# Attention stage of a three-stage kernel: 65-column products in two column halves, per-head fp32 projections on 64 rows, output transposes one step later

## The chip, the cores and the metric

The kernel runs on one core of a Trainium2 chip. The metric is the device time of one execution in microseconds; lower is better. The engines of a core have names of their own in the profile: PE is the matrix engine (TensorE), PEld its weight loads, DVE the vector engine, ACT the scalar engine, POOL GpSimd, and SP the engine whose queue issues nearly all DMAs here. PE's two operands are called stationary (loaded first, by a weight load) and moving (streamed through). An accumulator bank is one of the eight banks of PSUM, into which PE writes and from which DVE and ACT read.

## The reference, cut to what matters

Three stages follow each other: feature-map attention, a dense mixture of experts weighted by a Sinkhorn matrix, and a routed mixture of experts. Only the first is touched by the change.

```python
# batch 4, heads 8, seq 576, head_dim 64, features 128
def phi(x):
    proj = np.einsum('bhsd,df->bhsf', x, w_phi)
    proj = proj - np.max(np.abs(proj), axis=-1, keepdims=True)
    return np.concatenate([np.exp(proj), np.exp(-proj)], axis=-1)
q_p, k_p = phi(q), phi(k)
kv = np.einsum('bhsf,bhsd->bhfd', k_p, v)
z = np.sum(k_p, axis=2)
num = np.einsum('bhsf,bhfd->bhsd', q_p, kv)
den = np.einsum('bhsf,bhf->bhs', q_p, z)[..., None] + 1e-06
x = num / den            # then x goes to _moe_ref and _moe2_ref
```

## The kernel before

**Units, groups, chunks.** The attention stage is cut into 8 units (`NU`): one unit is two batches of one pair of heads, 1152 tokens. A unit has 9 chunks of 128 tokens, in `NG` = 5 groups (`CH`): four groups of two chunks and a last one of a single chunk. Chunk 4 holds the end of one batch and the start of the other.

**One step.** The main loop makes one `step` per group. In it the k side works on group i and the q side on a group four steps further back, so that the q side of a unit runs while the k side of the next unit does. The helpers a step calls, with their lines:

- `proj` (L144 to L164), once for k and once for q: projects the two heads of a pair at once. The features matrix stands twice on the diagonal of `wphi`, 256 columns wide. Inputs and matrix are split into a high and a low part (`split_in`, L116: ACT casts, POOL subtracts; `wbh`, `wbl`), and three fp32r products per chunk are added up: L151, L152, L153. DVE then takes the largest magnitude of each row and head (L155) and subtracts it (L157). On the k side ACT takes the two exponentials (L161).
- `kvm` (L166): products of the exponentials of k (stationary, 128 features) with v and a column of ones (moving, 65 columns: 64 and the sum z), per chunk, sign and head (L176). They accumulate in banks C and B over the unit; at its end ACT copies them out as `kvz` (L180).
- `qtr` (L183): transposes of the subtracted projections of q through PE (L190), into a bank D; ACT takes the exponentials from there (L192).
- `num` (L195): products of the exponentials of q (stationary, 128 tokens) with `kvz` (moving, 65 or 130 columns), into a bank D (L205). DVE adds a small number to the denominators (L219), inverts (L220) and multiplies (L223), which gives `xn`.
- `xtr` (L226): transposes `xn` through PE (L232) into a bank A, ACT copies it (L234), and SP writes it to DRAM (L236).

**Order within a step.** Each engine works its instructions off in the order in which the program issues them. Without a `turn` the order is `qtr`, `proj` of k, `proj` of q, `kvm`, then `xtr` for the group whose `num` was in the last step, then `num`. In one step of five (`turn`, where the last group of a unit is summed) `kvm` comes first and q is projected before k. In DVE's queue the two projections' work stands ahead of the division of the same step.

**Banks.** Tag A has 4 banks, D has 2, B and C one each; tiles of one tag take them in turn. `qtr` and `num` alternate on the two D banks, `proj` and `xtr` share the four A banks.

**End of the stage.** In the last four steps and the two that flush the pipeline (`tail`) there is no k work; q projections go to bank C, `xtr` to B, and pieces of the second stage's first products (`fill`, `p1_group`, L583, lines L429 to L431 with 384 columns) are put between.

Of the kernel before, what the change touches and what calls it, by code (L numbers as in the profile page):

```python
# [11 lines left out]
F32 = mybir.dt.float32  # L12
F32R = mybir.dt.float32r
# [3 lines left out]
ALU = mybir.AluOpType  # L17
# [27 lines left out]
def build(tc, a, out):  # L45
# [23 lines left out]
    def f32(ap):  # L69
        return ap.bitcast(F32)  # L70
# [28 lines left out]
    CH = [(0, 1), (2, 3), (4, 5), (6, 7), (8,)]  # L99
    S2 = 2 * S  # L100
    W = D + 1

    def load_in(u, which, g):
        bp, h_ = units[u]
        cs = slice(CH[g][0] * P, (CH[g][-1] + 1) * P)
        r = ap_.tile([P, 2 * P], F32, tag="r" + which, bufs=3, name=f"r{which}{u}{g}")
        SP.dma_start(out=r[:, 0:cs.stop - cs.start], in_=a[which + "T"][bp, h_, :, cs])
        live["r" + which, u, g] = r

# [3 lines left out]
        SP.dma_start(out=v, in_=a["v"][bp, h_])  # L113
        live["v", u] = v

    def split_in(u, which, g):  # L116
        r = live.pop(("r" + which, u, g))
        n = len(CH[g]) * P
        bufs = 3 if which == "k" else 2
        hi = ap_.tile([P, 2 * P], F32R, tag="h" + which, bufs=bufs, name=f"h{which}{u}{g}")  # L120
        lo = ap_.tile([P, 2 * P], F32R, tag="l" + which, bufs=bufs, name=f"l{which}{u}{g}")
        A.copy(hi[:, :n], r[:, :n])
        (V if u == 0 else G).tensor_tensor(out=lo[:, :n], in0=r[:, :n], in1=f32(hi[:, :n]), op=ALU.subtract)
        live["s" + which, u, g] = (hi, lo)

    def warm(n):
        ps = psum("D", [P, P])
        for _ in range(n):
            T.matmul(ps, ident, ident, start=True, stop=True)

    wphi = ap_.tile([P, 2 * P], F32, bufs=1, name="wphi")
    V.memset(wphi, 0.0)
    for g in range(2):
        SP.dma_start(out=wphi[g * D:(g + 1) * D, g * P:(g + 1) * P], in_=a["w_phi"])
    for g in range(3):
        load_in(0, "k", g)
    load_v(0)
    warm(10)
    wbh = ap_.tile([P, 2 * P], F32R, bufs=1, name="wbh")
    wbl = ap_.tile([P, 2 * P], F32R, bufs=1, name="wbl")  # L140
    V.tensor_copy(wbh, wphi)
    V.tensor_tensor(out=wbl, in0=wphi, in1=f32(wbh), op=ALU.subtract)

    def proj(u, which, g):  # L144
        hi, lo = live.pop(("s" + which, u, g))
        n = len(CH[g])
        ps = psum("C" if live.get("tail") else "A", [P, 2 * n, P])
        for c in range(n):
            o = ps[:, 2 * c:2 * c + 2, :].rearrange("p h f -> p (h f)")
            cs = slice(c * P, (c + 1) * P)  # L150
            T.matmul(o, hi[:, cs], wbh, start=True, stop=False)  # L151
            T.matmul(o, hi[:, cs], wbl, start=False, stop=False)  # L152
            T.matmul(o, lo[:, cs], wbh, start=False, stop=True)  # L153
        m = ap_.tile([P, 4], F32, tag="m", bufs=4, name=f"m{which}{u}{g}")[:, 0:2 * n]
        V.tensor_reduce(out=m, in_=ps, axis=AX.X, op=ALU.max, apply_absolute_value=True)  # L155
        pr = ap_.tile([P, 4, P], F32, tag="pr" + which, name=f"pr{which}{u}{g}")[:, 0:2 * n]
        V.tensor_tensor(out=pr, in0=ps, in1=m.unsqueeze(2).to_broadcast([P, 2 * n, P]), op=ALU.subtract)  # L157
        if which == "k":
            ek = ap_.tile([P, 4, 2, P], F32, tag="eq" if u == 0 and g == 2 else "ek", bufs=2, name=f"ek{u}{g}")
            for sg in range(2):  # L160
                A.activation(out=ek[:, 0:2 * n, sg, :], in_=pr, func=AF.Exp, scale=1.0 - 2.0 * sg)  # L161
            live["ek", u, g] = ek
        else:
            live["pr", u, g] = pr  # L164

    def kvm(u, g):  # L166
        v, ek = live["v", u], live.pop(("ek", u, g))
        if g == 0:
            live["kv", u] = [psum(t, [P, 2, 2 * W]) for t in "CB"]
        for sg in range(2):  # L170
            for ci, c in enumerate(CH[g]):
                o, w = (0, 2 * W) if c in (0, 4) else (0, W) if c < 4 else (W, W)
                s0 = 0 if c == 0 else c + 1 if c <= 4 else c + 2
                for h_ in range(2):
                    ps = live["kv", u][h_]
                    T.matmul(ps[:, sg, o:o + w], ek[:, 2 * ci + h_, sg, :], v[:, h_, s0 * W:s0 * W + w], start=(c == 0 and sg == 0), stop=(c == 8 and sg == 1))  # L176
        if g == len(CH) - 1:
            kvz = ap_.tile([P, 2, 2, 2 * W], F32, tag="kvz", name=f"kvz{u}")
            for h_, ps in enumerate(live.pop(("kv", u))):
                A.copy(kvz[:, h_], ps)  # L180
            live["kvz", u] = kvz
# [13 lines left out]
    def num(u, g):  # L195
        eq, kvz = live.pop(("eq", u, g)), live["kvz", u]
        n = len(CH[g])
        ps = psum("D", [P, 6 * W])
        off, at_ = 0, []
        for ci, c in enumerate(CH[g]):  # L200
            o, w = (0, W) if c < 4 else (W, W) if c > 4 else (0, 2 * W)
            at_.append((off, w))
            for h_ in range(2):
                for sg in range(2):
                    T.matmul(ps[:, off:off + w], eq[:, sg, h_, ci * P:(ci + 1) * P], kvz[:, h_, sg, o:o + w], start=(sg == 0), stop=(sg == 1))  # L205
                off += w
        d = ap_.tile([P, 4], F32, tag="d", name=f"d{u}{g}")
        xn = ap_.tile([P, 4, D], F32, tag="xn", name=f"xn{u}{g}")

        def views():  # L210
            if CH[g][0] == 4:
                for b in range(2):
                    yield slice(64 * b, 64 * b + 64), ps[64 * b:64 * b + 64, 0:4 * W].rearrange("p (h e) -> p h e", h=2)[:, :, b * W:b * W + W], slice(0, 2)
                yield slice(0, P), ps[:, 4 * W:6 * W].rearrange("p (h e) -> p h e", h=2), slice(2, 4)
            else:
                yield slice(0, P), ps[:, 0:2 * n * W].rearrange("p (h e) -> p h e", h=2 * n), slice(0, 2 * n)

        for p_, v_, s_ in views():
            V.tensor_scalar_add(d[p_, s_], v_[:, :, D], 1e-6)  # L219
        V.reciprocal(d[:, 0:2 * n], d[:, 0:2 * n])  # L220
        for p_, v_, s_ in views():
            k_ = s_.stop - s_.start
            V.tensor_tensor(out=xn[p_, s_, :], in0=v_[:, :, 0:D], in1=d[p_, s_].unsqueeze(2).to_broadcast([p_.stop - p_.start, k_, D]), op=ALU.mult)  # L223
        live["xn", u, g] = xn

    def xtr(u, g):  # L226
        bp, h_ = units[u]
        xn = live.pop(("xn", u, g))
        n = len(CH[g])
        ps = psum("B" if live.get("tail") else "A", [P, n * P])  # L230
        for c in range(n):
            T.transpose(ps[:, c * P:(c + 1) * P], xn[:, 2 * c:2 * c + 2, :].rearrange("p h e -> p (h e)"), ident)  # L232
        xo = ap_.tile([P, 2 * P], F32, tag="xo", name=f"xo{u}{g}")
        A.copy(xo[:, 0:n * P], ps)  # L234
        o = bp * S2 + CH[g][0] * P
        SP.dma_start(out=xd[:, h_, o:o + n * P], in_=xo[:, 0:n * P])  # L236


    for g in range(3):
        split_in(0, "k", g)  # L240
    ones = c0.tile([P, P], F32, name="ones")
    V.memset(ones, 1.0)
    trif = wp.tile([P, 1024], F32, tag="wA11_1", name="trif")[:, 0:P]
# [384 lines left out]
            if bg:  # L628
                bg.popleft()()

    dk, dq, dx = deque(), deque(), deque()
    filled = [0]

    def step(k, q, fill=None):
        qq, xq = list(dq), list(dx)
        dq.clear()
        dx.clear()
        if k:
            dk.append(k)
        kq = [dk.popleft() for _ in range(len(dk) - (2 if k and k[0] == 0 else 1 if k else 0))]  # L640
        turn = any(t[1] == len(CH) - 1 for t in kq)
        if turn:
            for t in kq:
                kvm(*t)
        for t in qq:
            qtr(*t)
        for which, t in (("q", q), ("k", k)) if turn else (("k", k), ("q", q)):
            if t:
                proj(t[0], which, t[1])
        if q:  # L650
            dq.append(q)
        if not turn:
            for t in kq:
                kvm(*t)
        if fill:
            filled[0] += 1
            next(fill)
        for t in xq:
            xtr(*t)
        if fill:  # L660
            filled[0] += 1
            next(fill)
        for t in qq:
            num(*t)
            dx.append(t)
# [7 lines left out]
    def at_(i):  # L673
        return order[i] if 0 <= i < len(order) else None

    for i in range((NU + 1) * NG - 1):
# [22 lines left out]
        if p == 5 and g == 3:  # L699
# [4 lines left out]
            ops = x_tasks(HS[0][1], q)  # L704
            ops["load"]()
            bg.extend(ops[k_] for k_ in XFIRST)
        for which, nx in (("k", at_(i + 1)), ("q", at_(i + 2 - NG))):
            if nx and not (which == "k" and i < 2):
                split_in(nx[0], which, nx[1])
        if i == NU * NG:  # L710
            while bg:
                bgpop()
# [4 lines left out]
        if p == 3 and g == NG - 1:  # L717
            misc_trans()
        bgpop()
    while dq or dx:  # L720
        step(None, None, first)
    at.close()

# [806 lines left out]
```

## Time and profile before

| what | value |
| --- | --- |
| median of 3 runs | 2019.83 us (2019.09 to 2023.27) |
| the profiled execution | 2022.27 us, its span in the trace 2020.5 us |
| mean granted TensorE clock over the span | 0.989 |
| PE busy | 1978.7 us (98%) |
| weight loads busy | 1901.4 us (94%) |
| DVE, ACT, POOL busy | 1309.5, 869.2, 995.1 us |
| attention stage (first to last product of `num` and `kvm`) | 10.5 to about 225 us |

An engine's busy time is the union of its instructions' durations. PE's instructions overlap: the duration of one product (about 0.27 us for a short one) holds its way through the array, and the next begins long before its end. What a product costs in a dense stretch is therefore the distance between the starts of two, not its duration. One fp32 product of the program shows as two records, each with a weight load of its own; a transpose and an fp32r product show as one.

### The profile page before, as it was taken

The numbers are of one execution on the slowest core, as the hardware profiler recorded it, in microseconds if no ns is written. First come the engines' busy times: TensorE is split into PE (matmuls) and PEld (weight loads), VectorE is DVE, ScalarE is ACT, GpSimd is POOL, SyncE is SP. The second block draws the span as 40 slices with busy tenths as digits, with TensorE's granted clock in tenths as the row PEclk, the third lists the DMA queues.
The fourth block names the chain that finished last, engine by engine and source line by source line (L and its number), as shares of the span: only waits on it lengthen the run. The fifth ranks groups of instructions, "written<-read, shape, count | busy, mean of one in ns | idle before, by whom it ended". The sixth has DMA issues, their size and how long they took to land.

```text
span 2020.5 us, 31417 instructions
## 1 busy us (share of the span) xinstructions
PE 1978.7 (98%) x11715; PEld 1901.4 (94%) x11715; DVE 1309.5 (65%) x1865; ACT 869.2 (43%) x1391; POOL 995.1 (49%) x733
## 2 busy tenths in 40 slices
PE   9999999999999999999999999999999998899998
PEld 9999999999999999999999999999999988778886
DVE  6766656466566656656665675666567444889996
ACT  5566432233333423333342333334233233777775
POOL 1255112575664747566474756647475432323332
PEclk9999999999999999999999999999999998999999
DMA  4344543543726345372644537364453344153851
GB/s 122 113 148 158 222 180 152 143 175 113 251 88 218 131 153 183 114 249 90 218 132 152 182 116 250 88 217 133 151 183 109 128 170 123 35 178 108 291 199 61
DMA packets 118979, 314.61 MB, mean 156 GB/s; under 512 B 11466, under 2 KB 65948, under 8 KB 118822
## 3 DMA queue, kind: packets, MB, share of 16 engines
q1 hardware_dynamic: 114726, 302.04, 44.8%
q0 software_dynamic: 4096, 10.51, 1.7%
q8 instruction: 95, 1.56, 0.3%
q14 instruction: 62, 0.51, 0.1%
HBM read 335.80 MB, written 32.28 MB: 182 GB/s over the span
## 4 chain that ended last, share of the span: by engine, by line
PE 76%; POOL 8%; DVE 6%; issue 5%; DMA 2%; ACT 2%; SPq 1%; POOLq 0%; DVEq 0%; ACTq 0%
PE Q L430 15%; PE Q L429 14%; PE Q L431 14%; PE psD L205 3%; PE psD L429 2%; PE psD L430 2%; PE psD L431 2%; POOL w1S L349 2%; PE psA L429 2%; PE psA L1140 2%; PE psA L431 2%; PE psA L430 2%; PE psA L1141 2%; POOL hB L477 2%; PE psA L1139 2%
## 5 line engine op out<-in xcount | busy, mean ns | idle before, releaser
L493 DVE TENSOR_TENSOR acca<-acca,Q 128x768 f32<-128x768 f32 x182 | 168.5, 949 | 133.3 <-PE Q L431 133.3
L429 PE MATMUL Q<-hT,w2S 128*128 128x384 f32 x468 | 157.5, 336 | 4.1 <-DVE rd L489 4.1
L477 POOL TENSOR_TENSOR hB<-rb,hB 128x768 fp32r<-128x768 f32 x39 | 72.1, 1848 | 180.4 <-ACT hB L474 180.4
L429 PE MATMUL Q<-xT,w1S 128*128 128x384 f32 x468 | 156.4, 334 | 0.9 <-ACT ra L498 0.9
L430 PE MATMUL Q<-hT,w2S 128*128 128x384 f32 x468 | 156.4, 334 | 0.0
L431 PE MATMUL Q<-hT,w2S 128*128 128x384 f32 x468 | 156.4, 334 | 0.0
L431 PE MATMUL Q<-xT,w1S 128*128 128x384 f32 x468 | 156.3, 334 | 0.0
L430 PE MATMUL Q<-xT,w1S 128*128 128x384 f32 x468 | 156.3, 334 | 0.0
L349 POOL TENSOR_TENSOR w1A<-raw,w1A 128x512 fp32r<-128x512 f32 x48 | 62.1, 1294 | 159.4 <-ACT w1A L348 86.2
L493 DVE TENSOR_TENSOR accb<-accb,Q 128x768 f32<-128x768 f32 x91 | 84.3, 949 | 68.0 <-PE Q L431 68.0
L1113 DVE TENSOR_TENSOR s1l<-rw,s1h 128x1024 fp32r<-128x1024 f32 x88 | 112.4, 1332 | 9.6 <-ACT s1h L1112 7.4
L489 DVE TENSOR_TENSOR Q<-Q,ra 128x768 f32<-128x768 f32 x39 | 37.7, 967 | 124.6 <-PE Q L431 124.6
L498 ACT COPY ra<-Q 128x768 f32<-128x768 f32 x39 | 31.3, 802 | 176.0 <-PE Q L431 156.3
L429 PE MATMUL Q<-xB,w1A 128*128 128x384 f32 x312 | 104.3, 334 | 0.7 <-DVE accb L851 0.7
L431 PE MATMUL Q<-hB,w2A 128*128 128x384 f32 x312 | 104.3, 334 | 0.0
L431 PE MATMUL Q<-xB,w1A 128*128 128x384 f32 x312 | 104.2, 334 | 0.0
L430 PE MATMUL Q<-xB,w1A 128*128 128x384 f32 x312 | 104.2, 334 | 0.0
L429 PE MATMUL Q<-hB,w2A 128*128 128x384 f32 x312 | 104.2, 334 | 0.0
L430 PE MATMUL Q<-hB,w2A 128*128 128x384 f32 x312 | 104.2, 334 | 0.0
L477 POOL TENSOR_TENSOR hT<-ra,hT 128x768 fp32r<-128x768 f32 x39 | 72.0, 1845 | 64.2 <-ACT hT L474 64.2
L477 POOL TENSOR_TENSOR hT<-rd,hT 128x768 fp32r<-128x768 f32 x39 | 72.3, 1854 | 57.0 <-ACT hT L474 57.0
L1079 POOL DMA_INDIRECT xgs<-x2d,idt x22 | 35.6, 1619 | 126.3 <-DVE gt L1077 126.0
(431 smaller groups left out, 6702.9 us busy)
## 6 DMA issues: line engine op xcount, KB each, us to landing
xT<-xpd SPq DMA_DIRECT2D x120, 768.0 KB
rw<-in_moe_w SPq DMA_DIRECT2D x176, 512.0 KB
xB<-xpd SPq DMA_DIRECT2D x90, 768.0 KB
raw<-in_moe_w SPq DMA_DIRECT2D x34, 512.0 KB
gate<-gd SPq DMA_DIRECT2D x45, 384.0 KB
rx<-in_moe_w SPq DMA_DIRECT2D x30, 512.0 KB
xpd<-xT SPq DMA_DIRECT2D x12, 768.0 KB
xpd<-xB SPq DMA_DIRECT2D x9, 768.0 KB
```

Of the source, the lines that this page charges most:

```text
L205: T.matmul(ps[:, off:off + w], eq[:, sg, h_, ci * P:(ci + 1) * P], kvz[:, h_, sg, o:o + w], start=(sg == 0), stop=(sg == 1))
L349: eng.tensor_tensor(out=t[:, 1], in0=r(nm), in1=f32(t[:, 0]), op=ALU.subtract)
L429: T.matmul(bank, w[:, 0, j, k, :], x[:, 0, k, :], start=start and k == 0, stop=False, skip_group_check=True)
L430: T.matmul(bank, w[:, 0, j, k, :], x[:, 1, k, :], start=False, stop=False, skip_group_check=True)
L431: T.matmul(bank, w[:, 1, j, k, :], x[:, 0, k, :], start=False, stop=stop and k == 1, skip_group_check=True)
L477: eng.tensor_tensor(out=hb[nm][:, 1], in0=src, in1=f32(hb[nm][:, 0]), op=ALU.subtract)
L489: V.tensor_tensor(out=out, in0=x, in1=y, op=op)
L493: V.tensor_tensor(out=z, in0=z, in1=ps, op=op)
L1113: V.tensor_tensor(out=lo, in0=r, in1=f32(hi), op=ALU.subtract)
L1139: T.matmul(ps[hf], th[:, k, :], wh[:, cs], start=(k == 0), stop=False)
L1140: T.matmul(ps[hf], tl[:, k, :], wh[:, cs], start=False, stop=False)
L1141: T.matmul(ps[hf], th[:, k, :], wl[:, cs], start=False, stop=(k == KD - 1))
```

## The change

Four things change in the attention stage. The products of `kvm` and `num` are issued in two halves of 64 stationary columns each (`HALVES`), which write to partitions 0 to 63 and 64 to 127 of the bank. The projections are plain fp32 products, one per chunk and head, on the 64 rows of that head; the split of inputs and matrix is gone, and each head has a bank of its own, so that DVE reads 256 columns at a time and twice as often. `xtr` moves from behind `kvm` to a place ahead of the projections, works on a group one step older (`late`; in the tail it doesn't wait a step), and takes a D bank. The raw inputs have four buffers for three, since the projection reads them itself.

```diff
     W = D + 1
+    HALVES = (slice(0, 64), slice(64, P))
 
     def load_in(u, which, g):
...
-        r = ap_.tile([P, 2 * P], F32, tag="r" + which, bufs=3, name=f"r{which}{u}{g}")
+        r = ap_.tile([P, 2 * P], F32, tag="r" + which, bufs=4, name=f"r{which}{u}{g}")
...
-    def split_in(u, which, g):
-        r = live.pop(("r" + which, u, g))
-        n = len(CH[g]) * P
-        bufs = 3 if which == "k" else 2
-        hi = ap_.tile([P, 2 * P], F32R, tag="h" + which, bufs=bufs, name=f"h{which}{u}{g}")
-        lo = ap_.tile([P, 2 * P], F32R, tag="l" + which, bufs=bufs, name=f"l{which}{u}{g}")
-        A.copy(hi[:, :n], r[:, :n])
-        (V if u == 0 else G).tensor_tensor(out=lo[:, :n], in0=r[:, :n], in1=f32(hi[:, :n]), op=ALU.subtract)
-        live["s" + which, u, g] = (hi, lo)
...
-    wphi = ap_.tile([P, 2 * P], F32, bufs=1, name="wphi")
-    V.memset(wphi, 0.0)
+    wphi = ap_.tile([P, P], F32, bufs=1, name="wphi")
     for g in range(2):
-        SP.dma_start(out=wphi[g * D:(g + 1) * D, g * P:(g + 1) * P], in_=a["w_phi"])
+        SP.dma_start(out=wphi[g * D:(g + 1) * D, :], in_=a["w_phi"])
...
-    wbh = ap_.tile([P, 2 * P], F32R, bufs=1, name="wbh")
-    wbl = ap_.tile([P, 2 * P], F32R, bufs=1, name="wbl")
-    V.tensor_copy(wbh, wphi)
-    V.tensor_tensor(out=wbl, in0=wphi, in1=f32(wbh), op=ALU.subtract)
 
     def proj(u, which, g):
-        hi, lo = live.pop(("s" + which, u, g))
+        r = live.pop(("r" + which, u, g))
         n = len(CH[g])
-        ps = psum("C" if live.get("tail") else "A", [P, 2 * n, P])
+        ps = [psum(t_, [P, n, P]) for t_ in ("CB" if live.get("tail") else "AA")]
         for c in range(n):
-            o = ps[:, 2 * c:2 * c + 2, :].rearrange("p h f -> p (h f)")
-            cs = slice(c * P, (c + 1) * P)
-            T.matmul(o, hi[:, cs], wbh, start=True, stop=False)
-            T.matmul(o, hi[:, cs], wbl, start=False, stop=False)
-            T.matmul(o, lo[:, cs], wbh, start=False, stop=True)
+            for h_ in range(2):
+                hs = slice(h_ * D, h_ * D + D)
+                T.matmul(ps[h_][:, c, :], r[hs, c * P:(c + 1) * P], wphi[hs, :], start=True, stop=True)
         m = ap_.tile([P, 4], F32, tag="m", bufs=4, name=f"m{which}{u}{g}")[:, 0:2 * n]
-        V.tensor_reduce(out=m, in_=ps, axis=AX.X, op=ALU.max, apply_absolute_value=True)
         pr = ap_.tile([P, 4, P], F32, tag="pr" + which, name=f"pr{which}{u}{g}")[:, 0:2 * n]
-        V.tensor_tensor(out=pr, in0=ps, in1=m.unsqueeze(2).to_broadcast([P, 2 * n, P]), op=ALU.subtract)
+        for h_ in range(2):
+            mh = m.rearrange("p (c h) -> p h c", h=2)[:, h_]
+            V.tensor_reduce(out=mh, in_=ps[h_], axis=AX.X, op=ALU.max, apply_absolute_value=True)
+            V.tensor_tensor(out=pr.rearrange("p (c h) f -> p h c f", h=2)[:, h_], in0=ps[h_], in1=mh.unsqueeze(2).to_broadcast([P, n, P]), op=ALU.subtract)
...
-                    T.matmul(ps[:, sg, o:o + w], ek[:, 2 * ci + h_, sg, :], v[:, h_, s0 * W:s0 * W + w], start=(c == 0 and sg == 0), stop=(c == 8 and sg == 1))
+                    for cs in HALVES:
+                        T.matmul(ps[cs, sg, o:o + w], ek[:, 2 * ci + h_, sg, cs], v[:, h_, s0 * W:s0 * W + w], start=(c == 0 and sg == 0), stop=(c == 8 and sg == 1))
...
-                    T.matmul(ps[:, off:off + w], eq[:, sg, h_, ci * P:(ci + 1) * P], kvz[:, h_, sg, o:o + w], start=(sg == 0), stop=(sg == 1))
+                    for cs in HALVES:
+                        T.matmul(ps[cs, off:off + w], eq[:, sg, h_, ci * P + cs.start:ci * P + cs.stop], kvz[:, h_, sg, o:o + w], start=(sg == 0), stop=(sg == 1))
...
-        ps = psum("B" if live.get("tail") else "A", [P, n * P])
+        ps = psum("D", [P, n * P])
...
+        if not live.get("tail"):
+            xq, late[:] = list(late), xq
+        else:
+            xq, late[:] = late + xq, []
...
         for t in qq:
             qtr(*t)
+        for t in xq:
+            xtr(*t)
...
+        if fill:
+            filled[0] += 1
+            next(fill)
         if not turn:
             for t in kq:
                 kvm(*t)
-        if fill:
-            filled[0] += 1
-            next(fill)
-        for t in xq:
-            xtr(*t)
...
-        for which, nx in (("k", at_(i + 1)), ("q", at_(i + 2 - NG))):
-            if nx and not (which == "k" and i < 2):
-                split_in(nx[0], which, nx[1])
```

## Rows read from the trace of the kernel before

**Rows 1.** Busy time by engine in stretches: length, then engine (instructions), clock, DMA share, GB/s.

```profile
70.00:95.00 25.00, 25.00 (x227) 25.00 (x226) 17.57 (x41) 15.19 (x39) 6.55 (x10) 1.00 0.35 105
...
195.00:228.00 33.00, 31.89 (x242) 31.36 (x241) 19.95 (x50) 17.91 (x42) 13.08 (x11) 1.00 0.30 108
```

**Rows 2.** Chain of waits in order of time: start, length, what sets the end.

```profile
100.24 1.73 PE psD L205 x16
105.80 1.74 PE psD L205 x16
...
125.30 1.73 PE psD L205 x16
...
204.42 1.73 PE psD L205 x16
...
209.67 1.73 PE psD L205 x16
```

**Rows 3.** Timeline of one full step on PE, and DVE's division in it: start, length.

```profile
100.08 1.90 PE L205 MATMUL psD<-kvz,eq 128*128 128x65 f32 x16
...
101.81 0.61 PE L190 MATMUL psD<-ident,prq 128*128 128x128 f32 x4
...
102.17 0.36 PE L151 MATMUL psA<-wbh,hk 128*128 128x256 f32 x1
...
102.53 0.15 DVE L219 TENSOR_SCALAR d<-psD 128x4 f32<-128x4 f32 x1
...
102.71 0.18 DVE L220 RECIPROCAL d<-d 128x4 f32<-128x4 f32 x1
...
102.92 0.42 DVE L223 TENSOR_TENSOR xn<-psD,d 128x256 f32<-128x256 f32 x1
...
103.27 0.68 DVE L155 TENSOR_REDUCE mk<-psA 128x4 f32<-128x512 f32 x1
...
103.68 0.39 PE L176 MATMUL psC<-v,ek 128*128 128x130 f32 x2
...
105.42 0.39 PE L232 MATMUL psA<-ident,xn 128*128 128x128 f32 x2
105.64 1.56 PE L205 MATMUL psD<-kvz,eq 128*128 128x65 f32 x13
```

**Rows 4.** Timeline of weight loads, third stage: eight products with 8 moving columns.

```profile
1639.93 1.03 PEld L897 LDWEIGHTS psC<-enT,acca 128*128 128x128 f32 x8
1640.88 0.19 PEld L429 LDWEIGHTS psD<-hT,w2A 128*128 128x128 f32 x1
```

**Rows 5.** Timeline of PE, third stage: two bf16 products and what follows.

```profile
1623.22 0.20 PE L931 MATMUL psC<-oh,tri 128*128 128x48 bf16 x1
1623.26 0.18 PE L932 MATMUL psC<-ohc,onesb 128*128 128x48 bf16 x1
1623.29 0.43 PE L429 MATMUL psA<-xB,w1S 128*128 128x384 f32 x1
```

**Rows 6.** Timeline of PE and loads around three transposes that use 16 rows.

```profile
232.35 0.34 PE L431 MATMUL psD<-hB,w2A 128*128 128x384 f32 x1
232.62 0.26 PEld L763 LDWEIGHTS psC<-ident,accb 16*128 16x128 f32 x3 [0.25 <-issue]
...
232.91 0.46 PEld L756 LDWEIGHTS psB<-xB,wgs 128*16 128x16 f32 x4
```

**Rows 7.** Instruction groups by shape, 0 to 420 us: busy, mean ns of one, idle before.

```profile
L123 POOL TENSOR_TENSOR lk<-rk,hk 128x256 fp32r<-128x256 f32 x28 | 20.6, 734 | 79.4 <-ACT hk L122 61.5 <-PE psD L205 11.2 <-PE psA L153 5.3
L223 DVE TENSOR_TENSOR xn<-psD,d 128x128 f32<-128x128 f32 x16 | 4.7, 292 | 0.5
L157 DVE TENSOR_TENSOR prk<-psA,mk 128x256 f32<-128x256 f32 x8 | 3.4, 425 | 0.8
L155 DVE TENSOR_REDUCE mk<-psA 128x2 f32<-128x256 f32 x8 | 3.3, 412 | 0.0
```

**Rows 8.** Waits, 5 to 228 us: who waited for whom, in total, times, longest.

```profile
DVE d L219 <- PE psD L205: 39.6, 31, 2.3
```

More of the change, by code (lines that the diff above doesn't have):

```diff
@@ L236, in xtr @@
         SP.dma_start(out=xd[:, h_, o:o + n * P], in_=xo[:, 0:n * P])
-    for g in range(3):
-        split_in(0, "k", g)
     ones = c0.tile([P, P], F32, name="ones")
@@ L629, in bgpop @@
                 bg.popleft()()
-    dk, dq, dx = deque(), deque(), deque()
+    dk, dq, dx, late = deque(), deque(), deque(), []
     filled = [0]
@@ L719, in build @@
         bgpop()
-    while dq or dx:
+    while dq or dx or late:
         step(None, None, first)
```

## The prediction

> **What bounds the kernel now.** I read the busy time by stretches first, then the chain of waits, then the timeline of one step, and last the shapes of instructions. In a steady unit PE and its weight loads are busy for all of the 25 us at the full granted clock of 2.4 GHz (1.00), DVE for 17.57 and ACT for 15.19 [rows 1]. The chain runs from `num` to `num`, 5.56 us apart for a full step, one in which all groups have two chunks; a whole unit of five steps takes 125.30 - 100.24 = 25.06 us [rows 2]. In the timeline the same full step falls into 16 records of `num`, 1.73 us; four transposes, 0.36; two projections of six products each, 102.17 to 103.68, 1.51; 16 records of `kvm`, 1.74; two output transposes, 0.22 [rows 3]. That is 5.56: PE is the bound and nothing else is. DVE waits for PE, 39.6 us in all ahead of the division alone [rows 8].
>
> What paces PE in the 65-column products is the weight load. A record of 65 or of 130 columns costs 0.108 us from start to start; eight products with only 8 moving columns cost 0.95 / 8 = 0.119 each [rows 4]. Eight columns or 65, the price is that of loading 128 stationary columns.
>
> **The split in halves.** Each record becomes two with 64 stationary columns: 64 records in a full step for 32. Call the price of one P. If loads of the two halves go one after the other, each costs half of the old one, P = 0.054, and nothing is won. If the two halves of the array load and work beside each other, the issue of instructions is the floor: two bf16 products with loads of their own follow each other after 0.04 and 0.03 us [rows 5], so P = 0.035. No row of this trace has a split product. I take 0.035: rows 5 show that PE can start products that closely, and the two halves share neither columns nor output partitions. Both ends stay for the range.
>
> **The projections.** Per chunk 3 records become 4 (two heads, two records each). At the old load price, R = 0.108, a full step pays 16 x 0.108 = 1.73 for 1.51. If the heads, on different rows, run side by side, R = 0.054 and it is 0.86. I take 0.054 by the same choice as for P; 0.108 stays as the other end. The casts on ACT and the subtractions on POOL (0.734 us each [rows 7]) vanish. I cost that at nothing: neither engine stands on a steady step's chain, and PE's full 25 us cover ACT's 15.19 and POOL's 6.55 [rows 1]. Inputs are now needed in their own step instead of the one before, with the same lead in the queue and a fourth buffer, so loads come no later than now; SP's order changes only in that the output's write stands one step later, two steps before the next stage asks for it.
>
> **Switches of the array's use.** Three transposes on 16 rows stand between full products: 232.35 to 232.91 is 0.56 us, less 0.18 for the product ahead and 3 x 0.06 for themselves, so some 0.2 for going in and out; the load wasn't pulled ahead and waited 0.25 [rows 6]. I take 0.1 for a switch. The new step has three: to 64 rows, to 64 columns, back to transposes. The Trainium skill (TensorEngine Tiling (Array Packing), Key Properties) says that a change of tiling mode drains the engine. Rows 6 agree for rows; for column halves no row shows it. Were a drain a product's whole way, 0.28, the sum below would be 0.18 x 35 steps = 6 us longer.
>
> **DVE.** It now takes each projection in two pieces. A reduction of 256 columns lasts 0.412 and a subtraction 0.425 [rows 7]; an instruction begins about 0.07 before the end of the one ahead (102.92 + 0.42 against 103.27 [rows 3]), so a pair costs 0.77. A full step has four, 3.08, and the division, 102.53 to 103.27, 0.74. DVE's own work grows to 3.82 of the step.
>
> **The moved transposes.** This is where a new wait arises. `qtr`, `xtr` and `num` now take the two D banks in turn, three per step. So `xtr` always gets the bank of the `num` just ahead of it, and must wait until DVE has divided out of it, though the data that it transposes are a step old. Before, `xtr` stood behind `kvm` in another bank. Behind the waiting `xtr` in PE's queue stand both projections, and for those waits DVE. On ACT the copy of `xtr` now stands ahead of k's exponentials, which `kvm` needs only a step later: no cost. So DVE, the engine with the growing work, idles in each step from the end of the division: 0.07 to that end, 0.05 for the signal (an estimate: 0.03 lies between dependent DVE instructions, 102.53 + 0.15 to 102.71 [rows 3], and across engines a little more), 0.22 transposes, 0.10 switch, five record distances of the first head's projection at 0.054, 0.27, and the last record's way, 0.28. Together 0.99.
>
> **The sum.** DVE's chain, full step: 3.08 + 0.74 + 0.99 = 4.81, against 5.56. PE's chain, from the last record of `num`: 0.28 its way, 0.04 signal, 0.81 division (the four transposes of `qtr` hide in these 1.13), 0.05, 0.22, two switches 0.20, 16 R and 64 P: 1.60 + 0.86 + 2.24 = 4.70. DVE's is the longer by a little. Two of the five steps have a one-chunk group: its pairs are about 0.50 (0.292 for a 128-column operation [rows 7], 0.28 for the reduction by an estimate along the same slope, less 0.07), so 2 x 0.77 + 2 x 0.50 + 0.74 + 0.99 = 4.27. The group with chunk 4 is divided in three pieces for one: 2 x 0.15 + 3 x 0.29 - 0.42 = 0.75 more. A unit: 3 x 4.81 + 2 x 4.27 + 0.75 = 23.7 for 25.06, -1.3; seven units, -9.3.
>
> First unit: it has only k work. 72 records of `kvm` at 0.11 become 144 at 0.035, 7.9 against 5.0 us; the load of v and DVE's longer pairs stand beside it, so between -2.9 and 0: I take -1.5. Tail: a full step is 5.25 [rows 2], of which 0.36, half of 1.51, 0.22 and 1.73 are known, leaving 2.18 for the inserted pieces. After: 1.13 + 0.05 + 0.22 + 0.20 + 8 x 0.054 + 2.18 + 32 x 0.035 = 5.33. The wait, which the inserted pieces covered before, eats what `num` gains. Six steps and the flush: +1, between -1 and +5. Sum: -9.8. Against the profiled execution's own 2022.27 us that is 2012.5; the runs' median lies 2.44 under that execution, which makes 2010.
>
> **The rivals.** *The halves don't overlap* (slower). P = 0.054: PE's chain in a full step is 1.60 + 3.46 + 0.86 = 5.92, or 6.79 with R = 0.108. A unit: five times 1.38 for wait, signal and switches, less 1.0 in the `turn` step, where `kvm` stands ahead and covers the wait; 1.0 for `xtr`; 72 R; 288 x 0.054 = 15.6; 0.75: 27.2 or 31.1, so +2.1 or +6.0, times seven +15 or +42; the tail adds 4 or 5. 2039 to 2067. It decides from P = 0.048 on, where 64 P eats the 3.10 us that a full step has for it. For it: the load's price goes by columns, and half the columns twice is the same. Against it: rows 5. The Trainium skill (TensorE: Matmul & The Clock Gate, The mechanism) has a weight load overlap with products in flight only where the row group differs; column halves share all rows, so by that rule it is this rival. The steady unit's loads and products, all on the same 128 rows and both busy for 25.00 us [rows 1], don't bear it out in that form.
>
> *The gain is given back* (no change). The halves overlap, yet R stays 0.108, where PE's chain is 1.60 + 1.73 + 2.24 = 5.57, the step of now; or P lies near 0.045. 2016 to 2024.
>
> *The wait doesn't bite* (faster still). If the bank were free in time, DVE's work alone would set the step, 3.82 and 3.28: a unit of 18.8, PE's 19 beside it, -6 each, about 1980. Against it: the order of banks in the program leaves no way round.
>
> **How the numbers follow.** Forecast 0.45, with its own range 2000 to 2017; halves without overlap 0.33; given back 0.15; wait that doesn't bite 0.07. Two runs of this kernel can be told apart from about 0.2%, 4 us. Faster: nine tenths of the first, the last, and a little of the third, 0.50. Same: the rest of the first and most of the third, 0.15. Slower: 0.35. The range leaves out the last case (0.07) and the upper part of the second, about 0.13: 1992 to 2046. The likeliest is 2010.
>
> **What would show it.** Right: starts of split records 0.03 to 0.04 us apart; PE idle ahead of `xtr` by some 0.7 us with DVE's division as the releaser; DVE above 75% in a steady unit, its idle time ahead of the first reduction; unit 23 to 25 us. Wrong: split records at 0.054 or more, projections at 0.108, or no idle time ahead of `xtr`.

## The result, and the profile after

The changed kernel takes 2037.67 us (2037.11 to 2038.38, four runs) beside 2019.93 for the kernel before on the same chip: ratio 1.0085, 95% interval 1.0067 to 1.0102. It is 17.7 us slower, where 10 us faster was forecast. The time lies inside the range given, on the side that the rival of the halves without overlap was to explain. That rival isn't what happened, so it is luck that the range holds: its upper part was there for another cause.

The page of the kernel after, two lines of it:

```profile
span 2036.0 us, 33944 instructions
...
PE 1956.4 (96%) x13011; PEld 1850.7 (91%) x13011; DVE 1321.3 (65%) x2012; ACT 848.5 (42%) x1311; POOL 947.4 (47%) x663
```

PE is busy for 22 us less than before and the span is 15.5 us longer: time has become idle time. The stretches show where. The first and the last line answer to [rows 1]; the middle one is one unit of five steps (columns as there).

```profile
70.00:95.00 25.00, 20.35 (x345) 17.06 (x341) 17.70 (x56) 11.67 (x26) 0.00 (x0) 0.93 0.32 97
...
76.64:104.14 27.50, 22.65 (x391) 19.34 (x391) 18.27 (x59) 12.30 (x27) 0.00 (x0) 0.94 0.43 131
...
195.00:228.00 33.00, 26.82 (x380) 22.26 (x380) 18.51 (x59) 16.65 (x35) 12.48 (x8) 0.95 0.47 170
```

PE was busy for all of 25 us; now it is for 20.35, and DVE for 17.70. Nobody is the bound: the two wait for each other in turn. The mean granted clock was 1.00 in these stretches before; now it is 0.93 to 0.95.

The timeline of the kernel after shows both halves of that (start, length; in brackets the idle time ahead and its releaser):

```profile
83.31 0.42 DVE L211 TENSOR_TENSOR xn<-psD,d 128x256 f32<-128x256 f32 x1
...
83.88 0.41 PE L220 MATMUL psD<-ident,xn 128*128 128x128 f32 x2 [0.45 <-DVE xn L211]
84.22 0.52 PEld L137 LDWEIGHTS psA<-wphi,rk 64*128 64x128 f32 x8 [0.17 <-issue]
84.22 0.71 PE L137 MATMUL psA<-wphi,rk 64*128 64x128 f32 x8
...
84.77 0.61 PE L137 MATMUL psA<-wphi,rq 64*128 64x128 f32 x8
84.96 0.42 DVE L142 TENSOR_REDUCE mk<-psA 128x2 f32<-128x256 f32 x1 [1.23 <-PE psA L137]
...
85.83 0.29 PE L163 MATMUL psC<-v,ek 128*64 128x65 f32 x4
...
86.17 0.29 PE L163 MATMUL psB<-v,ek 128*64 128x65 f32 x4
...
86.29 1.53 PE L193 MATMUL psD<-kvz,eq 128*64 128x130 f32 x32
...
87.75 0.33 PE L177 MATMUL psD<-ident,prq 128*128 128x128 f32 x1
...
90.13 0.44 PE L220 MATMUL psD<-ident,xn 128*128 128x128 f32 x2 [1.24 <-ACT eq L179]
...
100.74 0.39 PE L137 MATMUL psA<-wphi,rq 64*128 64x128 f32 x4
100.96 0.61 PE L137 MATMUL psA<-wphi,rk 64*128 64x128 f32 x8
101.51 1.15 PE L193 MATMUL psD<-kvz,eq 128*64 128x65 f32 x32
102.59 0.63 PE L177 MATMUL psD<-ident,prq 128*128 128x128 f32 x2
```

First the prices. 32 records of `num` with 65 columns take 102.59 - 101.51 = 1.08 us, 0.034 each on the average of the run (0.035 forecast, 0.108 before). Within the run they are closer: in the middle of `kvm` twelve records take 86.17 - 85.83 = 0.34, 0.028 each, and read record by record they start in pairs, two of them 0.007 us apart and the next two 0.05 later. The rest of the 1.08 is paid at the two ends of the run. Four projection records in the middle of a run take 100.96 - 100.74 = 0.22, 0.055 each (0.054); they too start in pairs. A whole projection of eight takes 0.54 or 0.55, about 0.11 more than 8 x 0.055. Record by record, this stands behind the transposes, between the first two pairs (0.21 apart, later pairs 0.11), and at the change to column halves (0.21 again); from one projection to the next nothing is paid. Where half of a group's 32 records have 130 columns, the run takes 87.75 - 86.29 = 1.46, so one of 130 columns costs (1.46 - 16 x 0.034) / 16 = 0.057: that one gains nothing by the split.

Then the wait. DVE divides at 83.31, the transposes of the older group start only at 83.88, the projections behind them at 84.22, and DVE sits idle for 1.23 us until their records are there. At 90.13 the same transposes wait for something else, for ACT's exponentials. That fits a bank from which ACT still reads the transposes of q of the same step; the trace names the releaser, not the bank. The waits of the kernel after between 20 and 245 us (us in total, times, longest):

```profile
DVE mk L142 <- PE psA L137: 32.6, 27, 1.6
...
PE psD L220 <- ACT eq L179: 18.2, 17, 1.9
PE psD L220 <- DVE xn L211: 16.6, 16, 1.9
...
DVE d L207 <- PE psD L193: 8.8, 9, 1.5
```

DVE's wait has moved from the division (39.6 us in [rows 8], and the same between 20 and 245 us; 8.8 now) to the first reduction. And in one unit, 76.6 to 104.1:

```profile
DVE mk L142 <- PE psA L137: 5.1, 4, 1.4
DVE mq L142 <- PE psA L137: 1.6, 1, 1.6
DVE d L207 <- PE psD L193: 0.8, 1, 0.8
DVE prk L143 <- ACT xo L222: 0.5, 1, 0.5
```

The clock is the last piece. In the step that ends a unit, `num` is over early, DVE still works on two projections, and PE is idle for 1.93 us, up to 77.42. Stretches of one microsecond of that step:

```profile
74.00:75.00 1.00, 1.00 (x28) 0.77 (x23) 0.97 (x4) 0.00 (x0) 0.00 (x0) 1.00 0.38 129
...
76.00:77.00 1.00, 0.00 (x0) 0.00 (x0) 0.90 (x5) 0.37 (x1) 0.00 (x0) 1.00 0.23 60
...
79.00:80.00 1.00, 1.00 (x10) 0.87 (x10) 0.72 (x2) 0.00 (x0) 0.00 (x0) 0.50 0.21 61
...
82.00:83.00 1.00, 1.00 (x32) 0.93 (x29) 0.18 (x2) 0.00 (x0) 0.00 (x0) 1.00 0.70 275
```

The granted clock falls from 2.4 GHz (1.00) to 1.2 (0.50) just after that pause, while PE is busy throughout, and is back in the last of these lines. What it costs can be read in this kernel by itself, from the starts of DVE's reciprocals in the step that follows the end of a unit: once with the fall, once, two units later, without.

```profile
76.64 0.18 DVE L208 RECIPROCAL d<-d 128x4 f32<-128x4 f32 x1
...
83.09 0.18 DVE L208 RECIPROCAL d<-d 128x4 f32<-128x4 f32 x1
...
133.47 0.18 DVE L208 RECIPROCAL d<-d 128x4 f32<-128x4 f32 x1
...
138.66 0.18 DVE L208 RECIPROCAL d<-d 128x4 f32<-128x4 f32 x1
```

6.45 against 5.19: 1.26 us for a fall. The pause of PE ahead of these two steps is the same:

```profile
77.42 0.30 PE L220 MATMUL psD<-ident,xn 128*128 128x128 f32 x1 [1.93 <-DVE xn L211]
...
134.26 0.30 PE L220 MATMUL psD<-ident,xn 128*128 128x128 f32 x1 [1.93 <-DVE xn L211]
```

So the pause alone doesn't decide. Of six such pauses at the ends of units five have a fall behind them, and of six shorter ones, 1.24 us ahead of `xtr` two steps later, two have. What else decides, no run tested. Read in stretches of two microseconds, the clock falls eight times between 50 and 220 us; in the kernel before it doesn't fall between 16 and 226 us.

The account, from the starts of the reciprocals: the first, the last of the seventh unit and the last of all, in the kernel before and in the kernel after.

```profile
26.35 0.18 DVE L220 RECIPROCAL d<-d 128x4 f32<-128x4 f32 x1
...
199.04 0.17 DVE L220 RECIPROCAL d<-d 128x2 f32<-128x2 f32 x1
...
225.09 0.17 DVE L220 RECIPROCAL d<-d 128x2 f32<-128x2 f32 x1
```

```profile
24.11 0.18 DVE L208 RECIPROCAL d<-d 128x4 f32<-128x4 f32 x1
...
211.02 0.17 DVE L208 RECIPROCAL d<-d 128x2 f32<-128x2 f32 x1
...
242.33 0.17 DVE L208 RECIPROCAL d<-d 128x2 f32<-128x2 f32 x1
```

The first division comes at 24.11 for 26.35: -2.2 (forecast -1.5). From there to the last of the seventh unit it takes 211.02 - 24.11 = 186.91 us, before 199.04 - 26.35 = 172.69: +14.2 (forecast -9.3). From there to the last division 242.33 - 211.02 = 31.31, before 225.09 - 199.04 = 26.05: +5.3 (forecast +1). Together +17.3. The -2.2 is not safely the change's: two kernels below with the same first unit have their first division at 21.44 and 22.17.

### The profile page after: what moved, and what is told of

It reads as the page before. It is cut to its first block, busy times and chain, and to the rows that moved or that the text cites. A ratio compares the mean times of both kernels' runs of the same rounds, so it can differ in the third digit from the quotient of the medians.

```text
span 2036.0 us, 33944 instructions
## 1 busy us (share of the span) xinstructions
PE 1956.4 (96%) x13011; PEld 1850.7 (91%) x13011; DVE 1321.3 (65%) x2012; ACT 848.5 (42%) x1311; POOL 947.4 (47%) x663
## 4 chain that ended last, share of the span: by engine, by line
PE 67%; POOL 9%; DVE 5%; issue 5%; ACT 1%; SPq 1%; DMA 0%; POOLq 0%; DVEq 0%; ACTq 0%
PE Q L416 14%; PE Q L417 14%; PE Q L415 14%; PE psD L415 2%; PE psD L416 2%; PE psD L417 2%; POOL w1S L335 2%; POOL hB L463 2%; PE psA L1127 2%; PE psA L1128 2%; PE psA L1126 2%; PE psD L1159 2%; PE psD L1161 2%; PE psD L1160 2%; PE psA L415 2%
## 5 line engine op out<-in xcount | busy, mean ns | idle before, releaser
L484 ACT COPY ra<-Q 128x768 f32<-128x768 f32 x39 | 31.3, 802 | 175.9 <-PE Q L417 156.2
L415 PEld LDWEIGHTS Q<-hT,w2S 128*128 128x128 f32 x468 | 87.8, 188 | 8.0 <-issue 7.9
```

The lines of the kernel that those rows point to most:

```text
L415: T.matmul(bank, w[:, 0, j, k, :], x[:, 0, k, :], start=start and k == 0, stop=False, skip_group_check=True)
```

## The experiments

Eight kernels ran. Each puts a part of the change into the kernel before, or takes one or more parts out of the changed one. All ratios are against the kernel before on the same chip (2020.3 to 2021.4 us), with their 95% intervals; a difference in us between two changed kernels is across chips, between which the kernel before differs by up to 1.5 us.

**The halves alone**, in the kernel before:

```diff
-    T.matmul(ps[:, off:off + w], eq[:, sg, h_, ci * P:(ci + 1) * P], kvz[...], ...)
+    for cs in HALVES:
+        T.matmul(ps[cs, off:off + w], eq[:, sg, h_, ci * P + cs.start:ci * P + cs.stop], kvz[...], ...)
```

(and the same in `kvm`).

> The kernel before with the split in column halves alone; projections, banks and the place of the output transposes stay as they were. Theory A (the halves pay, and what lost the time is the order of banks: the transposes' wait for the division): PE's full step falls from 5.56 by 3.47 and rises by 64 x 0.0345 = 2.2 and two switches of 0.1, to 4.5; DVE's work stays at 3.4, nothing new waits; a unit goes from 25.06 to about 20.7, seven units -30, first unit and tail -2 each: about 1986 us. Theory B (half the clock after PE's idle time is what lost it): the same sign, but PE is never idle long here, so the clock stays whole and the time is that of A. Theory C (the halves only move the wait to ACT's exponentials or DVE, whoever is next): 2010 or more.

Measured: 2005.88 us, ratio 0.9923 (0.9907 to 0.9938). The halves gain 15 us by themselves; the rival of halves without overlap is dead. They gained less than forecast. A steady unit is 21.7 to 22.6 us for the 20.7 expected, of which the 130-column records that keep their price make about 1.0 (an estimate: 24 pairs a unit at 0.11 for 0.07). Around 138 us the trace has a stall, and the clock is at half behind it, though theory B had it whole: ACT waits for a late input, and the exponentials that `num` needs stand behind that cast in ACT's queue (two lines of that timeline, and the stretch around it).

```profile
137.81 0.41 ACT L123 CAST hq<-rq 128x256 fp32r<-128x256 f32 x1 [2.85 <-DMA rq<-in_qT]
...
139.31 1.95 PE L208 MATMUL psD<-kvz,eq 128*64 128x65 f32 x26 [2.94 <-ACT eq L194]
```

```profile
120.00:145.00 25.00, 22.05 (x325) 19.99 (x320) 14.81 (x37) 17.14 (x43) 21.34 (x23) 0.87 0.64 209
```

Why that input was late (209 GB/s flow in this stretch, 118 between 45 and 70 us) no run tested.

**The old place of the output transposes, with the new bank**, in the changed kernel:

```diff
         for t in qq:
             qtr(*t)
-        for t in xq:
-            xtr(*t)
...
             for t in kq:
                 kvm(*t)
+        for t in xq:
+            xtr(*t)
```

> The changed kernel with one edit: the output transposes go back behind the k-v products, still in a D bank and still one step late. The bank that they then take was divided out of long before. Theory A: DVE's step is its own work, 4 x 0.79 + 0.83 = 4.0, with 0.1 to 0.3 of gap, PE's about 4.0; a unit of 20 to 21 us for the changed kernel's 27.5; seven units -45, about 1990 us, and PE's idle time and the half clock go with it. Theory B (the clock alone): the half clock goes, which is 1.3 us in each of seven units: about 2028. Theory C (DVE's work in twice as many pieces is the bound whatever the order): 2020 to 2030.

Measured: 2011.02 us, ratio 0.9948 (0.9933 to 0.9964). The sign is turned, but nearly half of the expected gain is missing. The wait went on to the next user of the bank: the transposes of q. In this kernel's timeline:

```profile
166.38 1.08 PE L177 MATMUL psD<-ident,prq 128*128 128x128 f32 x4 [2.34 <-DVE xn L211]
...
168.65 0.42 DVE L142 TENSOR_REDUCE mk<-psA 128x2 f32<-128x256 f32 x1 [2.42 <-PE psA L137]
```

Six such waits come to 14.0 us between 20 and 215 us, and the clock falls behind three of them. The stretch from the last division of the seventh unit to the last of all is back to 25.75 us from 31.31. At both places three tiles a step on two banks make someone wait for the division.

**Whole products in the changed kernel**, the other parts kept:

```diff
-                    for cs in HALVES:
-                        T.matmul(ps[cs, off:off + w], eq[:, sg, h_, ci * P + cs.start:ci * P + cs.stop], kvz[...], ...)
+                    T.matmul(ps[:, off:off + w], eq[:, sg, h_, ci * P:(ci + 1) * P], kvz[...], ...)
```

(and the same in `kvm`).

> The changed kernel with whole 65-column products again; the projections per head and the early transposes stay. Theory A: PE's chain of a full step becomes 1.6 + 0.3 + 0.9 + 32 x 0.108 = 6.2 and is longer than DVE's, a unit is 28 to 30 us at full clock: 2042 to 2055 us, slower than the changed kernel. If the halves themselves did the harm (theory D: switches of the array's use, or the half clock through less work on PE): 2037 or less.

Measured: 2064.11 us, ratio 1.0195 (1.0173 to 1.0217), 26 us above the changed kernel and above the 2042 to 2055 expected. So the halves are no reason for the loss. How much of the 26 us is theirs is less sure: the four executions go from 2055.5 to 2068.5 us, and the traced one, the slowest, is at half clock from 206 to 227 us besides three falls before. Its units take 28.3 to 31.3 us ahead of that. That `num` and `kvm` still count there, though PE idles, fits a step in which PE and DVE work in turn.

**More work for PE where it idles**: `num` of the turn step issued twice, with the same result.

```diff
-                for sg in range(2):
+                for sg in list(range(2)) * times:
...
-            num(*t)
+            num(*t, times=2 if turn else 1)
```

> The changed kernel, but in the one step of five where a unit is summed the numerator products are issued twice over (the first result is overwritten by the same one). They fill 1.1 of the 2.3 us for which PE stands idle there, before the clock halves. Theory B: the granted clock stays whole in most units, 1.3 us each are won: 2028 to 2031 us, though PE does more work. Theory A says nothing against it, but puts the larger part elsewhere. If the half clock costs nothing because DVE's chain hides it: 2037 to 2038, with the clock whole; if PE's added work delays the division: more.

Measured: 2035.41 us, ratio 1.0064 (1.005 to 1.0078), 2.3 us under the changed kernel, with intervals that overlap. It is a miss in the main: behind the turn the step is now mostly 5.19 us, but the falls have moved rather than gone, to six from eight after 20 us, and a step that holds one later in the unit lasts 6.98 for 5.40. Work beside the wait doesn't mend it. By the starts of the reciprocals the first division comes 1.9 us earlier, which this edit doesn't explain, the seven units are 1.7 shorter and the tail 0.8 longer. The idle time of PE that it aimed at is 1.93 us in the rows above, rather than the 2.3 expected.

**The new place, in a bank of tag A:**

```diff
-        ps = psum("D", [P, n * P])
+        ps = psum("D" if live.get("tail") else "A", [P, n * P])
```

> The changed kernel with one edit: before the tail the early output transposes take an A bank instead of a D bank; their place, ahead of the projections, stays. Theory A (the bank, not the place): their bank was read out in the step before, so they start as soon as q's transposes are through; DVE's gap of 1.1 to 1.4 per step shrinks to 0.3 or less, PE is never idle for 2 us and keeps its full clock; a unit of 27.5 falls to 20 to 22: 1988 to 2003 us. Theory E (the place: PE does the transposes while DVE has nothing, so DVE's gap stays at transposes, switch and the first projection, 1.1): 2020 or more.

Measured: 2014.94 us, ratio 0.9973 (0.9963 to 0.9982): the bank alone is worth 22.7 us, all of it in the seven units (164.1 us for 186.9); the tail, where the bank is still D, takes 31.29 for 31.31. The transposes run during the division, and after 20 us the clock falls once. But the unit is 24.08 us, not 20 to 22. Each step now takes five tiles of tag A, two for each projection and one for `xtr`, and there are four; the second projection waits for ACT's copy of `xtr`:

```profile
77.98 0.38 PE L220 MATMUL psA<-ident,xn 128*128 128x128 f32 x2
...
79.65 0.71 PE L137 MATMUL psA<-wphi,rq 64*128 64x128 f32 x6 [0.42 <-ACT xo L222]
```

Such waits come to 11.7 us in 28 steps between 20 and 200 us. The Trainium skill (TensorEngine Tiling (Array Packing), Gotcha 1: PSUM Pressure) says that different row tiles write to different banks, which makes row tiling press on PSUM; the trace agrees: two banks for a projection where there was one, five tiles a step on four banks, and this wait.

**Everything of the moved transposes undone**, halves and per-head projections kept: place and delay are those of the kernel before, and so is the bank up to the tail, where it stays D (before: B).

```diff
-        ps = psum("D", [P, n * P])
+        ps = psum("D" if live.get("tail") else "A", [P, n * P])
...
-        if not live.get("tail"):
-            xq, late[:] = list(late), xq
-        else:
-            xq, late[:] = late + xq, []
...
-        for t in xq:
-            xtr(*t)
...
         if not turn:
             for t in kq:
                 kvm(*t)
...
+        for t in xq:
+            xtr(*t)
```

> The changed kernel without its third part: output transposes at the old place, not late, in an A bank before the tail; the column halves and the projections per head stay. Theory A: like the run with the early transposes in an A bank, or a little better, since nothing stands between q's transposes and the projections: 1985 to 2003 us. If the projections in two pieces make DVE the bound (theory C): slower than the halves alone, 2006 or more, with DVE busy for over 95% of a steady unit.

Measured: 1999.3 us, ratio 0.9896 (0.9879 to 0.9912). It beats both kernels, by 21.0 and by 38.4 us. Two stretches and one reduction:

```profile
45.00:70.00 25.00, 22.37 (x401) 18.87 (x400) 22.12 (x76) 13.69 (x31) 0.58 (x1) 1.00 0.34 103
70.00:95.00 25.00, 23.41 (x429) 20.06 (x427) 20.73 (x67) 13.99 (x31) 0.00 (x0) 1.00 0.48 151
```

```profile
74.67 0.42 DVE L142 TENSOR_REDUCE mk<-psA 128x2 f32<-128x256 f32 x1 [0.38 <-PE psA L137]
```

DVE is busy for 88 and 83% of these stretches, a unit takes 22.5 us, the clock is full, and the idle time ahead of the first reduction is 0.38 us for 1.23. The stretch from the last division of the seventh unit to the last of all takes 24.68 us for 31.31. The wait of the second projection for ACT's copy is there too, but only six times between 20 and 200 us, 4.7 us in all. The Trainium skill (TensorEngine Tiling (Array Packing), PSUM Bottleneck) says that tiling speeds up TensorE but not the reading of PSUM, which may then become the limit. The trace goes that way, but not so far: DVE's share has risen from 70% [rows 1], and PE is still busy for 89 and 94%.

**The projections alone**: the kernel above with whole products, by the edit shown for the changed kernel (`HALVES` out of `kvm` and `num`).

> The changed kernel's projections alone: whole 65-column products, output transposes at the old place and in an A bank. Theory A: PE stays the bound; per chunk and side three records of 0.119 become four of 0.055, -0.137, eighteen times per unit, and two switches of 0.1 per step come in: 25.06 - 2.5 + 1.0 = 23.6, seven units -10: about 2010 us. Theory C (DVE's pieces cost more than PE gains): 2020 or more. If the two heads' products don't overlap when whole products stand around them: 2030.

Measured: 2023.84 us, ratio 1.002 (1.001 to 1.003); 2010 was expected, so this is a miss. The timeline of a full step says where the 0.65 us went that the faster records save:

```profile
101.57 0.52 PEld L137 LDWEIGHTS psA<-wphi,rk 64*128 64x128 f32 x8 [0.17 <-issue]
...
102.91 0.71 PE L137 MATMUL psA<-wphi,rq 64*128 64x128 f32 x6 [0.41 <-ACT xo L220]
...
103.54 0.49 PE L162 MATMUL psC<-v,ek 128*128 128x130 f32 x2
```

From the first projection to `kvm` it takes 103.54 - 101.57 = 1.97 us, where the six-product projections took 1.51 [rows 3]: two changes of the array's use and a wait for an A bank cost more than the records save. PE is still nearly full there (23.98 of 25 us between 70 and 95), so each of these shows. That they don't show beside the halves, because PE has slack there, is argued and not tested.

**The step's delay alone**, added to the version with everything of the moved transposes undone (e6 in the text below; e5 is the new place in a bank of tag A): `xtr` on the older group, at the old place, in an A bank.

```diff
+        if not live.get("tail"):
+            xq, late[:] = list(late), xq
+        else:
+            xq, late[:] = late + xq, []
```

> The kernel of e6_transposes_as_before with one thing added: the output transposes work on a group one step older, as in the changed kernel, at their old place behind kvm and in an A bank. Theory place: with the bank settled, what is left of the moved transposes' cost (e5, 2014.9, against e6, 1999.3) comes from their standing ahead of the projections, where their bank and ACT's copy come between two pairs of projection banks; lateness alone costs nothing: 1997 to 2003, a steady unit of 22.5 to 23.1 us. Rival, lateness: the older data keep their buffer and the flush of the pipeline is longer by a step, and this is the cost: 2008 or more, with the difference in the tail or in the units.

Measured: 1998.85 us, ratio 0.9885 (0.9868 to 0.9901), the same as without. The delay costs nothing; so the 16 us between the bank of tag A at the new place (2014.94) and this one come from the place ahead of the projections. About 11 lie in the seven units (164.1 us against 152.9), where the second projections' waits for A banks come to 11.7 us, and about 6 in the tail (31.3 against 25.7), where both kernels use a D bank. Whether the place would cost anything in the units with banks to spare wasn't run.

Two things were not tried: a bank for `xtr` that no other tile uses, at the new place (all eight are in use), and both heads of a projection in one bank, which would leave A banks over.

## Why the prediction was wrong, by its own steps

The step that failed is the sum over DVE's chain. It had 0.92 us of idle time a step behind the division, the full clock throughout, and +1 for the tail. The runs show 1.34 us a step of that wait (6.7 a unit), seven steps of the seven units with a fall of the clock, 9.4 us, and +5.3 in the tail.

**Price of a split record, price of a projection record: right, the first with some luck.** 0.034 and 0.055 for 0.035 and 0.054. That the halves and the heads work beside each other was right. But 0.035 was taken for a floor of the issue, and none shows at that height: records start 0.007 us apart in a pair and at 0.028 each within a run, and 0.034 is the average with the ends of the run. The rule of the Trainium skill that spoke against it (TensorE: Matmul & The Clock Gate, The mechanism: loads overlap products only where the row group differs) doesn't hold for these column halves: by it a pair would have kept about 0.108 us (an estimate: the whole record's price), and the trace has 0.068, or 0.057 within a run. The step missed the 130-column records, which keep 0.057 each.

**Switches: near.** 0.1 each was taken. Record by record it is 0.10 to the column halves, 0.10 back to transposes, and about 0.2 to the 64 rows, half of it between the first two pairs.

**The moved transposes: right in kind, too small.** That `xtr` would wait and DVE idle behind it was the forecast's own mechanism. "Always gets the bank of the `num` just ahead" was wrong: of the 33 waits of `xtr` in the rows above 16 end with the division and 17 with ACT's exponentials, which last longer still, so D's tiles can't have been taken in strict turn. DVE idles for 5.1 + 1.6 = 6.7 us per unit ahead of its first reduction, where 5 x 0.92 = 4.6 was in the sum: +2.1. In the step shown the division ends at 83.31 + 0.42 = 83.73 and the reduction starts 1.23 later: 0.15 to the transposes (0.05 forecast), 0.34 to the first projection record (0.32), and 84.96 - 84.22 = 0.74 from there (0.55). The last comes of the pairs: read record by record, the first head is through only with the fourth pair, 0.44 after the first record where 0.27 was taken.

**DVE's own work: right.** The unit without its 8.0 us of waits is 19.5 us; the forecast, 23.7 - 4.6 = 19.1.

**The clock: not in the sum.** The prediction took 1.00 throughout, though it made PE's chain (4.70) no longer the bound and put in a pause for PE in each step. Five of the steps behind a unit's end hold a fall, at 1.26 us each, and two other steps (116.64 to 123.61 and 144.30 to 151.27) one at 6.97 - 5.40 = 1.57: 9.4 us of the seven units.

The unit shown adds up: 23.7 + 2.1 of longer waits + 1.3 of clock + 0.4 of DVE's own = 27.5. The 1.3 are DVE's waits of 0.8 and 0.5 in the list for that unit: both lie in the step with the fall, and the step from 133.47 without one has neither. For the seven units the forecast is missed by 14.2 + 9.3 = 23.5 us, of which the clock is 9.4 and the rest, 2.0 a unit, the longer wait and small sizes. The division of the loss between wait and clock rests on such step lengths; the runs show that bank and place cause both, since with them undone the wait ahead of the first reductions falls from 6.7 to 1.8 us a unit and the clock doesn't fall after 20 us (1999.3 us).

**The tail: mis-sized.** +5.3 for +1. Its six steps wait in the same way, 6.0 + 2.3 us of `xtr` between 200 and 245 us, and the inserted products stand behind the waiting transposes rather than in front. The first step, 211.02 to 220.07, takes 9.05 us for 7.35 and also holds the eighth fall. Here it is the place and not the bank: with `xtr` behind `kvm` again and still in a D bank the same stretch takes 25.75 and 24.68 us, and with the place kept 31.29.

**The rivals.** The one with the right sign had the wrong cause: halves that don't overlap would have given nearly this time, but the halves alone are 15 us faster than the kernel before, and without them the changed kernel is 26 us slower. "The wait doesn't bite" can be set beside the kernels with halves, per-head projections and `xtr` in a bank of tag A before the tail, where it doesn't bite there: 2015, 1999 and 1999, not 1980. DVE's work alone doesn't set the step there either, since A banks and the handing over between engines remain (22.5 us a unit for 18.8).

**What would show it.** Split records 0.03 to 0.04 apart, PE idle ahead of `xtr`, DVE idle ahead of its first reduction: all seen, though the division is the releaser for only half of the waits ahead of `xtr`. DVE above 75% (66% in the unit shown) and a unit of 23 to 25 us (27.5): not. The mechanisms were there; a sum of two chains, taken each at its best and with a margin of 0.11 us between them, wasn't how the step came out.

## What to carry to other kernels

Ask of each part of a change by itself whether it pays: here the halves alone gain 15 us, halves and projections 21, and the moved transposes take 38. Try the parts together too: the projections alone lose 4 us, and beside the halves they gain about 6. When an edit makes the bounding engine faster, a tile that shares its bank with the result of the step just ahead can tie the two engines into one chain, and the loss can be larger than the wait as worked out: here 9.4 us of half clock came on top. Count the tiles per step against the banks of their tag before moving one; and where two engines end close to each other on paper (4.81 and 4.70 us here), expect more than the longer chain, since each handover between them counts.

## What the runs showed of the hardware

- Fp32 products with 64 stationary columns on alternating halves start 0.034 us apart on the average of a run of 32 with 65 moving columns (0.028 within a run, in pairs 0.007 apart), where a whole one takes 0.108; with 130 moving columns they start 0.057 apart.
- Fp32 products on 64 rows, two heads side by side, start 0.055 us apart.
- Changing from 64-row products to column halves, or from these to transposes, cost 0.10 us; from transposes to 64 rows it was about 0.2, with 0.17 of idle weight load; from one 64-row projection to the next nothing.
- The granted clock fell to 1.2 GHz behind five of six pauses of PE of 1.93 us and two of six of 1.24 us, so the length of the pause alone doesn't decide. The slower time lay behind the pause, under work that was then late: 1.26 us of a 6.45 us step.
